# Attention and a gated feed-forward block on one core: nine x tiles transposed by DMA instead of TensorE, and SP's queue in source order

## The chip, the core and the metric

The kernel runs on one core of a Trainium2 chip. A core has five engines that run side by side, each with a queue of its own that it works through in order: TensorE (PE in the profile, with its weight loads as PEld), VectorE (DVE), ScalarE (ACT), GpSimd (POOL) and SyncE (SP). They meet by semaphores: an instruction waits until another engine or a transfer has counted one up. Transfers between the chip's memory (HBM) and the core's (SBUF) are issued by SP, ACT or POOL and carried out by 16 DMA engines. TensorE writes to PSUM, from where VectorE or ScalarE fetch its results.

The metric is the device time of the kernel in microseconds. Before the change it is 335.49 us, the median of three runs (335.31 to 337.4).

## What is computed

Attention with a sliding window over q, k and v of (8 batches, 8 heads, 576 positions, 64), then a gated feed-forward block on its output:

```python
scores = q @ k.T / sqrt(64) + slope[h] * -(i - j)      # only where 0 <= i - j < 128
attn   = softmax(scores)                                # over j
x      = (attn @ v) transposed to (4608 tokens, 512)    # 512 = 8 heads x 64
g      = x @ w_gate                                     # 512 -> 1536
out    = (g * sigmoid(g) * (x @ w_val)) @ w_out         # 1536 -> 512
```

Inputs and output are float32; the matrix products are made in float16 with float32 sums.

## The kernel before

**Units and blocks.** The attention is cut into 36 units of 128 queries. Two batches make a super-unit of nine units (p = 0 to 8): four of the first batch, four of the second, and p = 8 for the last 64 positions of both. The rank of a k, q or v tile is the number of the unit whose positions it holds. Scores of a unit read the k tile of its own rank and the q tiles of its own and the next rank (the window reaches over two tiles); units p = 3 and 7 have no next tile in their batch, and p = 7 of a later super-unit also makes a part of the ninth unit and so reads q of p = 8. The feed-forward block runs over nine blocks of 512 tokens: block n takes x of four units (block 3 takes units 13 to 16, block 4 units 18 to 21, block 5 units 22 to 25), block 8 the four ninth units.

**One unit.** `scores(i)` makes products of k and q on TensorE (lines 289 and 325), ScalarE takes the exponential (295, 329), VectorE multiplies by the mask (301, 333). `weighted(i)` multiplies by v on TensorE (357) and VectorE divides by the sums (360, 361), which leaves x with tokens across the partitions. The feed-forward products need x, k and q with the feature across the partitions, so all three are transposed.

**Transposing.** q and k up to rank 10 go through TensorE (`transposed`, line 215) and are fetched from PSUM by VectorE or ScalarE; from rank 11 on (`QK_DMA_FROM`) SP issues one transposing transfer for each (line 236). x of units 0 to 21 goes through TensorE, four transposes into one PSUM tile (line 385), and is copied to xT by VectorE or ScalarE (387, 389); from unit 22 on (`X_DMA_FROM`) SP issues a transposing transfer (line 379).

**Loads.** POOL issues all loads of q, k and v (lines 188 and 182), in an order written out by hand: after unit i those of rank i+7. They land in natural tiles, five each for q and k, which come free when the transpose has read them; v has 12 tiles, kT 12 and qT 9 places. The x tiles number three, the xT tiles three.

**Feed-forward.** `gate_val` makes the gate and value products of blocks 0 to 5 (line 413), with an activation (431) and two products on VectorE (432, 443). The projection of block 0 is a plain product (`project`, 467, fetched by ScalarE at 471); that of the later blocks is made with seven products in place of eight (`strassen`, 548). A half block of it yields two output tiles: the last write of the first is VectorE's at line 553, that of the second ScalarE's at 589, and SP stores each of them (459). Blocks 6 to 8 make their gate products with seven products too (637).

**What sets the order.** `everything` interleaves steps of the feed-forward block with steps of the attention. A scheduler then places the instructions of an engine, except where the engine is put under `manual_schedule`: there they keep the order in which the source gives them. POOL is so from the start, TensorE in the first steps and from step 60 on (about 90 us), SP never. `ahead(i)`, called after `weighted(i)` and the loads, emits transposing transfers of q and k for the units to come, from a list `order` in which `need[i]` says how many entries unit i needs:

```python
            if not late or i == last:
                weighted(i)
                yield i
            loads_to(i + 7)
            ahead(i)
```

After that x of the unit is transposed; from unit 13 to 21 that is put off by one unit, so that TensorE need not wait for VectorE.

Of the kernel before, what the change touches and what calls it, by code (L numbers as in the profile page):

```python
# [16 lines left out]
P = 128  # L17
WIN = 128
QK_DMA_FROM = 11
X_DMA_FROM = 22  # L20
MASKS_AT = (3.0, 5.0, 6.0, 7.0)
ALONE = 8
MANUAL = "compute"
ET = mybir.EngineType
# [4 lines left out]
LEAD = 6  # L29
# [21 lines left out]
def kernel(  # L51
# [92 lines left out]
    def busy(n):  # L144

        t_ = ps_f.tile([P, 512], FP32, name="nil", tag="po", bufs=1)
        for _ in range(n):
            nc.tensor.matmul(t_, idle[:, 0:P], idle, start=True, stop=True)
# [13 lines left out]
    last = len(units) - 1  # L162
# [60 lines left out]
    order = []  # L223
# [4 lines left out]
    need = [18 * s + n for s in range(NSUP) for n in (3, 5, 7, 8, 11, 13, 15, 18 if s else 16, 18)]  # L228
# [108 lines left out]
    def weighted(i):  # L337

        s, p = units[i]
        x = xpool.tile([P, H, D], FP16, name="x", tag="x")  # L340
        xs[i] = x
        for half in range(2):
            pool, tag = (ps_f, "gv") if i < FIRST else (ps_a, "a")
            av = pool.tile([P, 4, D + 1], FP32, name="av", tag=tag)
            todo = []
            for j in range(4):
                h = 4 * half + j
                if p == 8:
                    for n, kt in enumerate((3, 7, 8)):
                        todo.append((j, ex[(s, "c", n)][:, slot(h), :], va[9 * s + kt][:, h, 0:D + 1]))  # L350
                else:
                    if p not in (0, 4):
                        todo.append((j, ex[(s, p - 1)][:, slot(h), 128:256],
                                     va[9 * s + p - 1][:, h, 0:D + 1]))
                    todo.append((j, ex[(s, p)][:, slot(h), 0:128], va[9 * s + p][:, h, 0:D + 1]))
            for n, (j, w, val) in enumerate(todo):
                nc.tensor.matmul(av[:, j, :], w, val, start=(n == 0), stop=(n == len(todo) - 1))  # L357
            rec = xpool.tile([P, 4, 1], FP32, name="rec", tag="rec", bufs=4)
            with tc.high_priority() if i in (6, 7) else ExitStack():
                nc.vector.reciprocal(rec, av[:, :, D:D + 1])  # L360
                nc.vector.tensor_mul(x[:, 4 * half:4 * half + 4, :], av[:, :, 0:D],  # L361
                                     rec.broadcast_to([P, 4, D]))
# [8 lines left out]
    def x_transposed(i):  # L371
        n, j = place(i)
        if n not in xT:
            xT[n] = bpool.tile([P, NKB, 512], FP16, name="xT", tag="xTc" if n == 8 else "xT",
                               bufs=1 if n == 8 else 3)
        x = xs.pop(i).rearrange("p h d -> p (h d)")
        dst = xT[n][:, :, j * P:(j + 1) * P]
        if i >= X_DMA_FROM:
            nc.sync.dma_start_transpose(dst, x)
            return  # L380
        pool, tag, n = ((ps_f, "gv", 3) if i == 2 else (ps_f, "po", 1) if i < FIRST
                        else (ps_a, "a", 4))
        pt = pool.tile([P, NKB, P], FP16, name="px", tag=tag, bufs=n)
        for kb in range(NKB):
            nc.tensor.transpose(pt[:, kb, :], x[:, kb * P:(kb + 1) * P], idm if i < FIRST else idm2)  # L385
        if i < FIRST:
            nc.vector.tensor_copy(dst, pt)
        else:
            nc.scalar.copy(dst, pt)
# [416 lines left out]
    loaded = done_t = 0  # L806

    def loads_to(r):
        nonlocal loaded
        while loaded <= min(r, NR - 1):  # L810
            load(loaded)
            loaded += 1

    def transposes_to(n):
        nonlocal done_t
        while done_t < n:
            transpose(done_t)
            done_t += 1

    def ahead(i):  # L820

        n = need[min(i + 4, last)]
        while done_t < n and order[done_t][1] < loaded and order[done_t][1] >= QK_DMA_FROM:
            transposes_to(done_t + 1)

    def run(steps):
        for fs in steps:
            for f in fs:
                f()
            yield  # L830
# [7 lines left out]
    def first_tiles():  # L838

        first_masks()  # L840
        transposes_to(1)
        begin_scores(0, 0, 0)
        transposes_to(2)
        begin_scores(0, 0, 1)
        transposes_to(need[0])
        begin_scores(0, 1, 0)
        begin_scores(0, 1, 1)
        begin_scores(1, 0, 0, ps_f, "gv", 3)
        for n, _ in enumerate(run(scores(0))):
            if n == 0:  # L850
                begin_scores(1, 0, 1, ps_f, "gv", 3)
                transposes_to(need[1])
        for i in range(FIRST):
            if i + 1 < FIRST:
                for n, _ in enumerate(run(scores(i + 1))):
                    if n == 0 and i == 0:
                        begin_scores(2, 0, 0)
                        begin_scores(2, 0, 1)
                    if n == 0 and i + 2 < FIRST:
                        transposes_to(need[i + 2])  # L860
            else:
                later_masks()
                for m in range(2):
                    wide(0, m, "g", P)
            weighted(i)
            if 0 < i < FIRST - 1:
                x_transposed(i - 1)
        x_transposed(2)
        begin(4, 2)
        x_transposed(3)  # L870
        begin(4, 3)

    def attention():

        waiting = []
        transposes_to(need[FIRST])
        for _ in run(scores(FIRST)):
            yield FIRST
        for i in range(FIRST, last + 1):
            late = i >= LATE  # L880
            if i < last:
                transposes_to(need[i + 1])
                for n, _ in enumerate(run(scores(i + 1))):
                    yield i - len(waiting)
                    if n == 2 and late:
                        weighted(i)
                        yield i - len(waiting)
# [5 lines that stand above are left out]
            yield i - len(waiting)  # L893
            if late and i < X_DMA_FROM:
                if waiting:
                    x_transposed(waiting.pop(0))
                waiting.append(i)
                yield i
                yield i
                continue  # L900
            while waiting:
                x_transposed(waiting.pop(0))
            x_transposed(i)
            yield i
            yield i + 1
# [9 lines left out]
    queue = ExitStack()  # L915
# [40 lines left out]
    loaded = 11  # L956
# [3 lines left out]
    done = n_att = 0  # L960
# [16 lines left out]
    def progress(steps):  # L977
        total = 0.0
        for size in steps:
            total += size  # L980
            yield total

    def everything():
        nonlocal done
        base = 0
        busy(WARM)
        with tc.manual_schedule(engines=ENGINES[MANUAL]):
            first_tiles()
            done = FIRST
            steps = progress(ffn())  # L990
            while (at := next(steps)) < ALONE:
                if at == 2.0:
                    nc.scalar.copy(idm2, idm)
                if at in MASKS_AT:
                    make_mask(MASKS_AT.index(at))
        fixed = ExitStack()
        for step in steps:
            if step >= FIXED_FROM and fixed is not None:
                fixed.enter_context(tc.manual_schedule(engines=ENGINES["pe"]))
                fixed, held = None, fixed  # L1000
            b1 = 24 + 3 * PRE

            lead = LEAD if done < 22 else LEAD + 4
            blk = (0 if step + LEAD < b1 else 1 if step + LEAD < 60
                   else min(NBLK - 1, 2 + int((step + lead - 60) // 34.5)))
            if step < b1:

                target = base + 1.25 * max(0, step - ALONE) + 1.5 * max(0, step - 16)
            elif step < 60:
                target = base + 32 + SECOND * 8 * (step - b1) / (60 - b1)  # L1010
            else:
                target = 84 + (step - 57) * RATE / 34.5
            most = n_att + 2 if step >= 60 else 1000
            while (n_att < min(target, most) or done < ready[blk]) and att_step():
                pass
        held.close()

    everything()
    queue.close()

# [29 lines left out]
```

## Time and profile before

| | |
|---|---|
| median of three runs | 335.49 us (335.31 to 337.4) |
| span of the profiled execution | 333.9 us, first to last instruction, 7719 instructions |
| between that span and the median | 1.6 us |
| granted TensorE clock | full, in all of the span |
| attention | ends at about 226 us, when the last x goes out |
| blocks 2, 3, 4, 5 begin on TensorE at | 90.0, 128.5, 166.1, 202.8 us |
| TensorE's transposes of x, line 385 | 88 instructions, 14.1 to 148.5 us |
| ScalarE's copies to xT, line 389 | 18, 585 ns each |
| SP's transposing transfers | 25 of k, 25 of q, 14 of x |

The page of the profile gives for each engine its busy time and its share of the span, then the span in 40 slices of 8.35 us with a digit for the busy tenths. PEclk is the clock that TensorE was granted. The DMA row is the mean busy share of the 16 DMA engines. In a list of waits a row reads: the instruction that waited and its line, the arrow, what ended the wait, then the total in us, how often, and the longest. In a timeline a row reads: start in us, length in us, engine, line, operation, output and inputs, shape, and how many instructions are merged. SP's instructions bear a q, since they only issue; how long a transfer takes is told apart, from issue to landing.

### The profile page before, as it was taken

Reading aid. Unit: us, or ns where it says so; the run is one execution under the profiler, and the core shown is the slowest. Engines: PE = TensorE matmul, PEld = TensorE weight load, DVE = VectorE, ACT = ScalarE, POOL = GpSimd, SP = SyncE. Lnnn points to the kernel's source line nnn. Section 1 sums busy time; section 2 is a strip of 40 time slices with the busy share of each in tenths; the row PEclk is TensorE's granted clock in tenths of the full one; section 3 lists DMA queues with packets and bytes.
Section 4 is the critical chain, followed back from the end, with each engine's and each line's share of the span. In section 5 each row is a group of like instructions: output and inputs, shape, how many; then the busy total and the mean of one; then the engine's idle time right before and its main releaser. Section 6 shows DMA issues by size and latency. Waiting matters only on the chain.

```text
span 333.9 us, 7719 instructions
## 1 busy us (share of the span) xinstructions
PE 325.9 (98%) x2955; PEld 218.5 (65%) x2955; DVE 274.2 (82%) x643; ACT 206.9 (62%) x413; POOL 111.0 (33%) x138
## 2 busy tenths in 40 slices
PE   8999999999999999999999999999999999999994
PEld 4665465544465655656655655666788888888883
DVE  4678878999797879988999999999855985775683
ACT  4976777464766657567456465563567667776650
POOL 8977776458964098551035000000000000000000
PEclk9999999999999999999999999999999999999999
DMA  9999999999999999999969532030100101011014
GB/s 154 175 179 175 177 185 164 122 142 184 141 170 159 140 195 162 160 168 155 179 128 152 117 34 81 16 96 17 65 29 36 64 2 65 25 41 65 0 65 127
DMA packets 161669, 37.64 MB, mean 113 GB/s; under 512 B 149472, under 2 KB 157280, under 8 KB 161632
## 3 DMA queue, kind: packets, MB, share of 16 engines
q0 software_dynamic: 118880, 18.62, 78.8%
q1 hardware_dynamic: 42064, 17.90, 27.8%
q10 hardware_dynamic: 688, 0.62, 0.6%
q8 instruction: 23, 0.38, 0.5%
q14 instruction: 14, 0.11, 0.1%
HBM read 37.91 MB, written 9.44 MB: 142 GB/s over the span
## 4 chain that ended last, share of the span: by engine, by line
PE 87%; DVE 8%; ACT 2%; issue 1%; DVEq 0%
PE po L548 19%; PE pg L413 17%; PE pv L413 16%; PE gX L637 9%; PE av L357 5%; PE gY L637 5%; PE ps L289 3%; PE p L548 3%; PE gZ L637 2%; DVE uu L432 2%; PE psc L325 2%; DVE hT L443 2%; PE po L467 2%; PE px L385 2%; DVE ex L301 1%
## 5 line engine op out<-in xcount | busy, mean ns | idle before, releaser
L413 PE MATMUL pv<-xT,wv_sb 128*128 128x512 f16 (+2 forms) x312 | 76.6, 363 | 0.3 <-DVE uu L432 0.2
L413 PE MATMUL pg<-xT,wg_sb 128*128 128x512 f16 (+2 forms) x324 | 76.5, 355 | 0.1
L431 ACT ACTIVATE tt<-pg 128x512 f16<-128x512 f32 x68 | 40.9, 603 | 44.6 <-PE pg L413 44.6
L295 ACT ACTIVATE ex<-ps 128x512 f16<-128x512 f32 x96 | 50.0, 608 | 7.4 <-PE ps L289 7.4
L432 DVE SCALAR_TENSOR_TENSOR uu<-tt,pg 128x512 f16<-128x512 f16 x67 | 45.6, 681 | 8.6 <-ACT tt L431 8.3
L443 DVE TENSOR_TENSOR hT<-uu,pv 128x512 f16<-128x512 f16 x68 | 46.2, 681 | 1.6
L182 POOL DMA_DIRECT2D va<-in_v_dram x40 | 34.5, 871 | 38.2 <-DMA out_dram<-osb 20.4
L548 PEld LDWEIGHTS <-hT 128*128 128x128 f16 x384 | 37.2, 98 | 10.7 <-issue 0.8
L413 PEld LDWEIGHTS <-wg_sb 128*128 128x128 f16 x324 | 28.5, 98 | 23.5 <-issue 2.2
L413 PEld LDWEIGHTS <-wv_sb 128*128 128x128 f16 x312 | 27.8, 98 | 24.4 <-issue 2.3
L188 POOL DMA_DIRECT2D kn<-in_k_dram x39 | 33.5, 863 | 18.8 <-DMA qT<-qn 6.2
L188 POOL DMA_DIRECT2D qn<-in_q_dram x39 | 33.6, 871 | 9.7 <-DMA va<-in_v_dram 4.7
L548 PEld LDWEIGHTS <-S 128*128 128x128 f16 x288 | 27.5, 98 | 7.5 <-issue 1.4
L301 DVE TENSOR_TENSOR ex<-ex,m_reg 128x1024 f16<-128x1024 f16 x42 | 28.5, 685 | 3.0 <-ACT ex L295 3.0
L361 DVE TENSOR_TENSOR x<-av,rec 128x256 f16<-128x256 f32 x72 | 28.5, 420 | 0.5
L548 PE MATMUL po<-T,S 128*128 128x256 f16 x192 | 25.9, 273 | 0.3 <-ACT u2s L574 0.3
L548 PE MATMUL po<-T,hT 128*128 128x256 f16 x192 | 26.0, 272 | 0.0
L329 ACT ACTIVATE exc<-psc 128x512 f16<-128x512 f32 x40 | 21.4, 608 | 3.2 <-PE psc L325 3.1
L691 DVE TENSOR_TENSOR hT<-s,v 128x512 f16<-128x512 f16 x18 | 7.6, 424 | 17.7 <-ACT s L690 17.7
L357 PEld LDWEIGHTS <-ex 128*128 128x128 f16 x384 | 17.5, 98 | 4.4 <-issue 1.0
L357 PE MATMUL av<-va,ex 128*128 128x65 f16 x384 | 19.3, 193 | 0.3 <-ACT ex L295 0.3
L289 PE MATMUL ps<-qT,kT 64*128 64x256 f16 x192 | 16.0, 272 | 0.9 <-DVE qT L220 0.6
(129 smaller groups left out, 534.1 us busy)
## 6 DMA issues: line engine op xcount, KB each, us to landing
out_dram<-osb SPq DMA_DIRECT2D x32, 256.0 KB, 2.4
va<-in_v_dram POOLq DMA_DIRECT2D x32, 128.0 KB, 6.9
qn<-in_q_dram POOLq DMA_DIRECT2D x31, 128.0 KB, 7.9
kn<-in_k_dram POOLq DMA_DIRECT2D x31, 128.0 KB, 7.3
wg_sb<-in_moe_w_gate_dram POOLq DMA_DIRECT2D x6, 256.0 KB, 7.6
wo_sb<-in_moe_w_out_dram POOLq DMA_DIRECT2D x3, 512.0 KB, 8.2
wv_sb<-in_moe_w_val_dram POOLq DMA_DIRECT2D x5, 256.0 KB, 7.6
kn<-in_k_dram POOLq DMA_DIRECT2D x8, 64.0 KB, 6.4
```

What stands on the lines that cost most here:

```text
L182: nc.gpsimd.dma_start(va[rank][p0:p1, :, 0:D], src)
L188: nc.gpsimd.dma_start(t_[p0:p1], src)
L295: nc.scalar.activation(e[:, o:o + 2, :], banks[q4][par], AF.Exp, scale=scale)
L301: nc.vector.tensor_mul(e[:, o, :], e[:, o, :], reg[:, o, :])
L357: nc.tensor.matmul(av[:, j, :], w, val, start=(n == 0), stop=(n == len(todo) - 1))
L361: nc.vector.tensor_mul(x[:, 4 * half:4 * half + 4, :], av[:, :, 0:D], rec.broadcast_to([P, 4, D]))
L413: nc.tensor.matmul(ps[:, c0:c1], w[:, kb, ms], xT[n][:, kb, c0:c1], start=(kb == 0 and c0 == 0), stop=(kb == NKB - 1 and c1 == 512), skip_ ...
L431: nc.scalar.activation(tt, pg[:, c0:c1], AF.Tanh, scale=0.5)
L432: nc.vector.scalar_tensor_tensor(out=uu, in0=tt, scalar=one if (n, m) == PIN else 1.0, in1=pg[:, c0:c1], op0=ALU.add, op1=ALU.mult)
L443: nc.vector.tensor_mul(hT[n][:, m, c0:c1], acted[(n, m)][1][:, c0:c1], pv[:, c0:c1])
L548: nc.tensor.matmul(dst, a[:, m, cols], b[:, m, :], start=(start and m == 0), stop=(m == HM - 1), skip_group_check=True)
L637: nc.tensor.matmul(dst[:, i, :], w[:, kb, c0 + i * P:c0 + (i + 1) * P], a[:, kb, :], start=(start and i == 0 and kb == 0), stop=(i == 1 an ...
```

## The change

Three edits. x of units 13 to 21 is transposed by a transfer from SP's queue, where TensorE and ScalarE did it. `ahead(i)` emits q and k of whole ranks up to i+4, where it emitted the entries that the scores of unit i+4 need. And from unit 12 on SP's instructions keep the order of the source, where the scheduler placed them. A constant in `everything` (22) is replaced by `X_DMA_FROM`, by which the number of steps that the attention is held ahead of a block becomes 10 instead of 6 for units 13 to 21 (from 22 on it was 10 already).

```diff
 QK_DMA_FROM = 11
-X_DMA_FROM = 22
+X_DMA_FROM = 13
+AHEAD = 4
+QUEUE_FROM = 12
...
     def ahead(i):
 
-        n = need[min(i + 4, last)]
-        while done_t < n and order[done_t][1] < loaded and order[done_t][1] >= QK_DMA_FROM:
+        while (done_t < len(order) and order[done_t][1] <= min(i + AHEAD, loaded - 1)
+               and order[done_t][1] >= QK_DMA_FROM):
             transposes_to(done_t + 1)
...
         for i in range(FIRST, last + 1):
             late = i >= LATE
+            if i == QUEUE_FROM:
+                queue.enter_context(tc.manual_schedule(engines={ET.SP}))
             if i < last:
                 transposes_to(need[i + 1])
...
-            lead = LEAD if done < 22 else LEAD + 4
+            lead = LEAD if done < X_DMA_FROM else LEAD + 4
```

`x_transposed(i)` branches on `X_DMA_FROM`: at and above it, it is one `nc.sync.dma_start_transpose(dst, x)`. The branch of `attention` that puts x off by one unit holds for units from 13 up to `X_DMA_FROM`, so it is not taken any more.

## The prediction

> **What bounds the kernel now.** I read the page's busy times first, then its slices, then the waits of TensorE, then those of SP's queue.
>
> ```profile
> PE 325.9 (98%) x2955; PEld 218.5 (65%) x2955; DVE 274.2 (82%) x643; ACT 206.9 (62%) x413; POOL 111.0 (33%) x138
> ...
> PEclk9999999999999999999999999999999999999999
> DMA  9999999999999999999969532030100101011014
> ```
>
> TensorE is busy for 325.9 of 333.9 us at full clock; nothing else is near its whole span. The DMA row says that transfers are dense up to about 180 us and thin after that. In the list of TensorE's own waits no row is longer than 1.2 us in total, and that one is the start of the kernel; the only wait for a transposed q or k is this:
>
> ```profile
> PE ps L289 <- DVE qT L220: 0.6, 2, 0.4
> ```
>
> So the time is the sum of what stands in TensorE's queue. An edit gains what it takes out of that queue, and loses what makes TensorE wait. SP's queue is where waiting happens now, at no cost:
>
> ```profile
> SPq L236 <- DMA kn<-in_k_dram: 85.7, 20, 55.2
> SPq L459 <- DVE osb L553: 84.3, 11, 11.8
> ```
>
> The first row is SP waiting for k to be loaded before it can transpose it (one of these waits, 55.2 us, is the start), the second is SP waiting for an output tile.
>
> **What is removed.** x of units 13 to 21 is transposed by four TensorE instructions each, 36 in all, and a ScalarE copy each, 9 in all. One instruction's row says 219 ns, but they overlap; what counts is how far the next one is pushed. TensorE's timeline:
>
> ```profile
> 104.25 1.03 PE L413 MATMUL pv<-xT,wv_sb 128*128 128x512 f16 x4
> 105.12 0.39 PE L385 MATMUL px<-idm,x 128*128 128x128 f16 x4
> 105.34 0.82 PE L548 MATMUL po<-wo_sb,S 128*128 128x256 f16 x6
> ```
>
> From the start of the four to the start of the next group it is 0.22 us. At the other units it is the same: 0.23 at 98.57 us, 0.22 at 111.91, 118.27, 124.81, 130.93 and 135.98, 0.23 at 142.45 and 148.33. Nine times 0.22 to 0.23 is **2.0 us off TensorE**, all on the path, since nothing is waited for there. The nine copies (585 ns each, 5.3 us of ScalarE) gain nothing: ScalarE is busy 62% and its longest wait is for TensorE (44.6 us).
>
> [...] The rows above show 0.056 us per block in a full queue. [...]
>
> **What is added.** Nine transposing transfers on SP (about 1.2 us of SP's time each, 10.8 us). SP then has three per unit of about 6 us, 3.6 us, and about 0.7 us of stores: it fits. Their landing is far from its reader. Block 3 begins at 128.54 us on TensorE and reads x of units 13 to 16; x of unit 16 is ready at 111.4 us, goes out at about 113 behind q and k of rank 20, and at the slowest landing in the trace, 8.9 us, is there at 122. Block 4 begins at 166.07 and its last x (unit 21) is ready at 142.1. So 6 us and more are spare; cost nothing, and if that cover went, the gate products of block 3 would wait for the difference. The x tiles (three) are free again well before their third successor three units later.
>
> **What is moved: SP's queue.** The built queue of the changed kernel runs, from rank 17 on: q and k of rank r, then x of unit r-4, and between these the two stores of each half block. In the built queue of before, x of unit 22 stands behind k of rank 33; now it stands behind rank 26. The source's own limit changes by one rank at most; it is the scheduler's hoisting that goes. Instructions of POOL stand in the same order, those of TensorE too but for the 36 transposes, so the new `lead` moves nothing there.
>
> What is now queued behind a waiting instruction: a store waits for its output tile, and behind it stand q and k of the next rank, which the scores three units on read. I take for each rank the moment that releases SP, add SP's issues (1.3 us a transposing transfer with its gap, 0.5 to 0.6 a store), and compare with the start of the first scores that need q. The two rows that matter most, release and need, on VectorE and TensorE:
>
> ```profile
> 124.89 0.41 DVE L553 SCALAR_TENSOR_TENSOR osb<-po,u2s 128x256 f32<-128x256 f32 x1
> ...
> 137.16 0.96 PE L289 MATMUL ps<-qT,kT 64*128 64x256 f16 x8
> ```
>
> - q of rank 23 (unit 22 reads it): tile ready 125.3; store, k22, q22, x of 18, store, so q23 goes out at 130.3. Need 137.16: 6.9 us. Need moves forward by seven removed groups, release by four: **6.2 us** are left for the landing.
> - q of rank 26 (unit 25): the ScalarE output copy at line 589 ends at 148.05; store, k26, so q26 goes out at 149.9. Need 156.07; less one removed group: **5.9 us**.
> - The others the same way, release first: q17 (output copy at line 471 ends at 88.3), out 90.2, need 99.76, less one group: 9.3. q20 (line 589 at 109.9), out 110.5, need 120.11, less two: 9.2. q24 (behind q23, k23 and x of 19), out 134.2, need 143.64, less three: 8.8. q29 (line 589 at 165.9), 166.5 to 174.7: 8.2. q32 (185.4), 186.0 to 192.1: 6.1. q35 (202.5, then k35), 204.4 to 210.3: 5.9.
>
> Against these stands the time from issue to landing:
>
> ```profile
> DMA to landing us min/median/max: 2.4/6.5/8.9
> ```
>
> This is line 236 as a whole. In parts: 6.3 to 8.9 (median 7.6) at 128 to 140 us, while POOL issues loads without a break; 2.5 to 4.8 at 57 to 62 and 3.5 to 5.2 at 156 to 160, when POOL stands still; x of units 27 to 35 lands in 2.4 to 4.0. q32 and q35 come when the loads are over (the last lands at 185.4): no stall. The ranks with more than 8 us cannot stall either. Only q23 and q26 are open. Bounds: at 2.4 us nothing, at 8.9 us 2.7 + 3.0 = **5.7 us of stall**; below nothing there is no end, since TensorE has no such wait now that could go.
>
> I take **about 5 us, so no stall**, and this is the choice that the forecast hangs on. The natural tiles of q and k have five buffers, so the load of rank r waits until rank r-5 is transposed. In before the transposes run far ahead (k of rank 23 goes out at 111.75, when TensorE has just scored unit 17), so POOL runs ahead too and seven loads are in flight at 130 us. Now, when q23 goes out, rank 22 has not landed, so the loads of rank 27 can't have begun, and those up to 26 have been out since about 119 to 127 us. That is nearer to the rows with POOL at rest. The same bursts that SP sends after a store find the loads held back by the very ranks that are late. The price of it, later loads, is covered: a load lands within 8 us (median of q), and rank r's load starts about two units before SP comes to it.
>
> **The sum**, against the profiled execution: span 333.9 - 2.0 + 0 = 331.9 us. The median of the runs, 335.49, lies 1.6 us above that span, which I leave as it is: **333.5 us**, 0.6% faster. About 1% is what a measurement of this kernel can tell from no change, so this counts as the same.
>
> **Rivals.**
> 1. *Part of the gain is eaten.* q23 and q26 land in 6.5 to 7.1 us, as the loaded rows' lower half. Stall at 7: 0.8 + 1.1 = 1.9, time 335.4. For it: the median of line 236 is 6.5. Against: the loads held back.
> 2. *Slower: the two stores hold back q23 and q26 in a full DMA queue.* The mechanism is the one above, with landing at 8.9 us at both: -2.0 + 5.7 = +3.7, **339.2 us**. It is slower than before from a landing of 7.1 us on. For it: nine more transfers of 128 KB in a stretch whose DMA row is all nines, and 8.9 was seen with 7 loads and 4 transfers of SP in flight. Against: the bytes that are added are 1.2 of 37.64 MB, and loads no longer run ahead.
> 3. *The change does less than it says.* The 36 transposes are gone from the built queue, so this can only be that they cost nothing where they stood: 335.5. The timeline speaks against it at nine places.
>
> **The numbers.** Forecast 0.60 (its own range 333.0 to 334.3), first rival 0.20 (334.3 to 336.0), second 0.15 (from 336.0 up, 339.2 at its price), third 0.05. Of the second I put 0.09 above 338.8, which is slower by over 1%. Faster by over 1% means below 332.1; TensorE's whole list of waits has little more to give, 0.03, out of the forecast's share. The range 332.8 to 337.5 leaves out a few hundredths below, and some 0.11 above, where the bound of 339.2 lies.
>
> **What would show it.** TensorE's px group has 52 instead of 88 instructions, the ScalarE copy at that place 9 fewer; 23 x transfers. Right: no wait of TensorE for a q or k transfer at the scores of units 22 and 25, landings of 4 to 6 us around 130 and 150 us, POOL waiting for transposed q and k between ranks. Wrong: a row of TensorE's weight loads or scores waiting for the transfer into qT, of 1 to 3 us, near 135 and 154 us. What would make the forecast wrong altogether is a landing above 7 us there, or a stall at places where I found over 8 us.

## The result and the profile after

The changed kernel takes **334.02 us** (median of 16 runs, 333.72 to 335.22), the kernel before 335.59 us (16 runs, 334.94 to 337.4). The ratio is 0.9947, with a 95% interval of 0.9932 to 0.9963: a gain of 1.6 us (by the interval 1.2 to 2.3), clear of noise. The forecast was 333.5 us in a range of 332.8 to 337.5. The gain that it named was 2.0 us; 1.6 came. It also held that about 1% is the least that can be told from no change; with 16 runs on each side half of that could be told.

First the busy times and the DMA row of the page of the changed kernel (its line numbers are two higher than before), which answer to those of before:

```profile
PE 324.5 (97%) x2919; PEld 216.6 (65%) x2919; DVE 273.4 (82%) x643; ACT 202.5 (61%) x404; POOL 111.1 (33%) x138
...
DMA  9999999999999999999999664231100101011014
```

TensorE has 36 instructions fewer and 1.4 us less of busy time, ScalarE has lost its nine copies and 4.4 us of busy time. The DMA row stays dense for two slices longer: what was loaded early is loaded later now. The spans of the two profiles (333.9 and 333.0) can't be subtracted as they stand, because the profiled execution of the changed kernel was 0.62 us later already when its first transposes were done, long before anything that the change touches. What counts is how the distance between the two moves after that.

At the place that the prediction showed, TensorE's timeline of the changed kernel reads:

```profile
104.65 1.03 PE L415 MATMUL pv<-xT,wv_sb 128*128 128x512 f16 x4
105.51 0.82 PE L550 MATMUL po<-wo_sb,S 128*128 128x256 f16 x6
106.17 1.03 PE L415 MATMUL pg<-xT,wg_sb 128*128 128x512 f16 x4
```

From the start of the value products to that of the projection it is 0.86 us; before, with the four transposes between, 1.09. Laid side by side, instruction by instruction, the two TensorE queues differ in time by these steps after the start, and by no other as large:

| where (time before) | step of the changed kernel against before |
|---|---|
| nine groups of four transposes, 98.6 to 148.3 us | -0.22 us each, -2.0 in all |
| scores of unit 22, 137.2 us | +0.65 us |
| scores of unit 25, 156.3 us | +0.24 us |
| scores of unit 28, 175.3 us | -0.24 us |
| sum | -1.4 us |

The second row is a wait that the prediction did not see. TensorE's timeline of the changed kernel there, then VectorE's, then VectorE's before:

```profile
135.26 1.03 PE L415 MATMUL pv<-xT,wv_sb 128*128 128x512 f16 x4
136.22 0.39 PE L291 MATMUL ps<-qT,kT 64*128 64x256 f16 x4
137.12 0.72 PE L291 MATMUL ps<-qT,kT 64*128 64x256 f16 x4 [0.51 <-DVE x L363]
```

```profile
135.49 0.41 DVE L505 TENSOR_TENSOR S<-hT 128x512 f16<-128x512 f16 x1
135.83 0.68 DVE L335 TENSOR_TENSOR exc<-exc,m_reg 128x1024 f16<-128x1024 f16 x1
136.43 0.24 DVE L362 RECIPROCAL rec<-av 128x4 f32<-128x4 f32 x2
136.63 0.76 DVE L363 TENSOR_TENSOR x<-av,rec 128x256 f16<-128x256 f32 x2
```

```profile
136.71 0.24 DVE L360 RECIPROCAL rec<-av 128x4 f32<-128x4 f32 x2
136.92 0.76 DVE L361 TENSOR_TENSOR x<-av,rec 128x256 f16<-128x256 f32 x2
```

The scores need four PSUM tiles, and the pool has four. Two of them still hold the sums of unit 20, which VectorE has yet to divide; it does so from 136.6 to 137.4 us, after other work that stands before it in its queue. TensorE came 0.94 us earlier than before, VectorE's division only 0.29, and the second half of the scores waits: the group takes 1.62 us, from 136.22 to 137.84. Before, the same scores took 0.96 us where 0.61 is their length without a wait, so 0.35 us of this wait was there already. It stood in the list of the weight loads, as one of the two waits of this row (at 137.7 us; the other, at 175.3, is at the scores of unit 28):

```profile
PEld L289 <- DVE x L361: 0.5, 2, 0.2
```

The third row is the landing of q of rank 26. It went out at 149.4 us and landed 155.7; the second half of unit 25's scores, which read it, could have begun at about 155.6. TensorE's timelines show the group at 0.87 us in the changed kernel, at 0.62 before, and at 0.65 in a second profiled execution of the changed kernel ("changed, measured again" in the experiments), in which the same q went out at 148.3 us and landed at 154.3, just in time:

```profile
155.34 0.87 PE L327 MATMUL psc<-qT,kT 64*128 64x128 f16 x16
156.07 0.62 PE L325 MATMUL psc<-qT,kT 64*128 64x128 f16 x16
154.16 0.65 PE L327 MATMUL psc<-qT,kT 64*128 64x128 f16 x16
```

The fourth row is a wait of before, again for VectorE's x, that has gone. The scores of unit 28 in the changed kernel, before, and in the second execution of the changed kernel:

```profile
174.20 0.70 PE L291 MATMUL ps<-qT,kT 64*128 64x256 f16 x8
174.71 0.94 PE L289 MATMUL ps<-qT,kT 64*128 64x256 f16 x8
172.81 0.93 PE L291 MATMUL ps<-qT,kT 64*128 64x256 f16 x8
```

The third and the fourth row belong together: where TensorE has lost 0.24 us at unit 25, it comes to unit 28 that much later and finds x divided; where q of rank 26 lands in time, neither step is there. The second execution has neither and ends as the first does: from the first of the nine groups to the end TensorE gains 1.35 us on before in it, 1.38 in the first. So the late q costs nothing in the end, and what is lost of the 2.0 us is the second row.

In SP's queue the waits have the same two heads as before:

```profile
SPq L461 <- DVE osb L555: 94.2, 13, 11.8
SPq L238 <- DMA kn<-in_k_dram: 61.4, 4, 55.5
```

SP now waits for a load of k only four times, where it was 20: it comes to q and k when they have long been there. POOL waits in its place. This is from POOL's list of waits, the changed kernel and then before, and below it the landing of q and k over the whole run of the changed kernel:

```profile
POOL kn L190 <- DMA kT<-kn: 31.4, 13, 4.7
POOL kn L188 <- DMA kT<-kn: 1.8, 1, 1.8
```

```profile
DMA to landing us min/median/max: 2.4/5.4/8.4
```

Thirteen loads of k were held back until the transposing transfer of five ranks earlier had freed a tile, and the median of the landing fell from 6.5 to 5.4 us.

### The profile page after: what moved, and what is told of

Its sections match the earlier page's. It is cut to its first block, busy times and chain, and to the rows that moved or that the text cites. A ratio compares the mean times of both kernels' runs of the same rounds, so it can differ in the third digit from the quotient of the medians.

```text
span 333.0 us, 7659 instructions
## 1 busy us (share of the span) xinstructions
PE 324.5 (97%) x2919; PEld 216.6 (65%) x2919; DVE 273.4 (82%) x643; ACT 202.5 (61%) x404; POOL 111.1 (33%) x138
## 4 chain that ended last, share of the span: by engine, by line
PE 85%; DVE 10%; ACT 2%; issue 1%; DVEq 0%
PE po L550 18%; PE pg L415 16%; PE pv L415 15%; PE gX L639 9%; PE gY L639 5%; PE av L359 5%; PE ps L291 3%; PE p L550 3%; DVE uu L434 2%; PE gZ L639 2%; DVE hT L445 2%; PE psc L327 2%; PE po L469 2%; DVE ex L303 1%; ACT tt L433 1%
## 5 line engine op out<-in xcount | busy, mean ns | idle before, releaser
L550 PEld LDWEIGHTS <-hT 128*128 128x128 f16 x384 | 37.1, 98 | 10.7 <-issue 0.8
```

The source lines that it names most:

```text
L550: nc.tensor.matmul(dst, a[:, m, cols], b[:, m, :], start=(start and m == 0), stop=(m == HM - 1), skip_group_check=True)
```

## Experiments

All ratios are to the kernel before, run beside each kernel on the same chip, with 95% intervals.

| kernel | median us | ratio |
|---|---|---|
| changed (first measurement) | 334.02 | 0.9947 (0.9932 to 0.9963) |
| queue alone | 335.22 | 0.9993 (0.9983 to 1.0002) |
| x alone | 348.27 | 1.0378 (1.0360 to 1.0396) |
| both ways | 335.86 | 1.0006 (0.9991 to 1.0021) |
| x of 20 and 23 early | 333.41 | 0.9949 (0.9926 to 0.9972) |
| lead of six | 334.10 | 0.9951 (0.9932 to 0.9969) |
| lead of three (two runs) | 356.12 | 1.0604 (1.0541 to 1.0666) |
| x of 20 early, lead of five | 332.81 | 0.9910 (0.9886 to 0.9934) |
| changed, measured again | 333.74 | 0.9946 (0.9926 to 0.9966) |

### SP's order without the x transfers

```diff
-X_DMA_FROM = 13
+X_DMA_FROM = 22
```

> SP's queue in source order and q and k whole ranks up to i+4, as in the changed kernel, but x of units 13 to 21 still transposed on TensorE. My theory (the gain is the 36 transposes that left TensorE's queue; the order of SP's queue is worth nothing by itself): the time of before, ratio 0.998 to 1.002, and TensorE's steps as in before. Rival (the order of SP's queue makes the gain): the time of the changed kernel, ratio 0.995. Both: fewer loads in flight than in before when q of ranks 23 and 26 go out, so their landing below 6.5 us.

Measured 335.22 us, ratio 0.9993, an interval that holds 1. TensorE's queue is that of before, and so is its time; no step of more than 0.1 us shows between the two after the start. q and k land in 3.9 to 5.3 us (median 4.7) between 128 and 140 us, against 6.3 to 8.9 before. So SP's order makes transfers faster that nobody waits for, and gains nothing by itself.

### The x transfers without SP's order

```diff
-            if i == QUEUE_FROM:
-                queue.enter_context(tc.manual_schedule(engines={ET.SP}))
...
-        while (done_t < len(order) and order[done_t][1] <= min(i + AHEAD, loaded - 1)
-               and order[done_t][1] >= QK_DMA_FROM):
+        n = need[min(i + 4, last)]
+        while done_t < n and order[done_t][1] < loaded and order[done_t][1] >= QK_DMA_FROM:
             transposes_to(done_t + 1)
```

> x of units 13 to 21 by transfer, but SP's order left to the scheduler and the old limit in ahead. x of unit 13 then stands behind k and q of rank 22 in SP's queue. My theory: it goes out at about 113 to 116 us instead of 93, x of unit 16 needs its tile (three x tiles), so VectorE is held for 3 to 6 us from 111 us on, and TensorE with it: 336 to 341 us, slower than the changed kernel by 2 us or more, ratio to before 1.00 to 1.02. Rival (x is wanted so late that any order will do): 334.0, ratio 0.995.

Measured 348.27 us: slower than the changed kernel by 14 us, where 2 to 7 were expected. The direction and the place were right, the size was not. SP's timeline has the first x of the nine (unit 13, ready at 92 us) at last here:

```profile
114.98 1.22 SPq L238 DMA_TRANSPOSE qT<-qn  x1
116.29 1.22 SPq L381 DMA_TRANSPOSE xT<-x  x1
```

It stood behind k and q of rank 23, whose loads SP had to wait for. VectorE's timeline shows the price, since x of unit 16 is to be written where x of unit 13 still lay, and TensorE's shows who waits for VectorE:

```profile
109.61 0.24 DVE L362 RECIPROCAL rec<-av 128x4 f32<-128x4 f32 x2
120.35 0.76 DVE L363 TENSOR_TENSOR x<-av,rec 128x256 f16<-128x256 f32 x2 [10.49 <-DMA xT<-x]
```

```profile
112.00 0.39 PE L291 MATMUL ps<-qT,kT 64*128 64x256 f16 x4
120.83 0.93 PE L291 MATMUL ps<-qT,kT 64*128 64x256 f16 x4 [8.44 <-DVE x L363]
```

VectorE waited 16.0 us in three such places. Another 3.1 us were lost to TensorE's clock after the long wait (below). So the two parts of the change belong together: the transfer is worth 2.0 us on TensorE, and it costs far more if x stands behind q and k that are not wanted yet.

### The transposes put back on TensorE, the transfers kept

```diff
-            if late and i < X_DMA_FROM:
+            old = xs[i]
+            x_transposed(i)
+            if late and i < 22:
                 if waiting:
-                    x_transposed(waiting.pop(0))
-                waiting.append(i)
...
+                    on_tensor(waiting.pop(0))
+                waiting.append(old)
...
```

`on_tensor` makes four transposes on TensorE into a PSUM tile that nobody reads.

> The changed kernel with the 36 transposes put back on TensorE: x of units 13 to 21 goes by transfer and is read from there, and TensorE transposes it as well, at the place of before, into a PSUM tile that nobody reads. SP's queue is that of the changed kernel; ScalarE is spared the nine copies. My theory (TensorE's time is the gain): the time of before, ratio 0.998 to 1.002. Rival (the gain comes from SP's order, or from ScalarE's nine copies of 0.585 us): 334.0, ratio 0.995.

Measured 335.86 us, ratio 1.0006. With the transposes back in TensorE's queue the gain is gone, though SP's queue is that of the changed kernel and ScalarE still has no copies to make. The gain is TensorE's time and nothing else. The steps of 0.24 us at the scores of units 25 and 28, one up and one down, are there in this kernel too (q of rank 26 landed at 156.06 us, the group took 0.88), so they don't come from the transposes that left TensorE. Nor does SP's order make them by itself: in queue alone that q landed in 2.4 us and neither step is there.

### VectorE's x of units 20 and 23 first

```diff
-            with tc.high_priority() if i in (6, 7) else ExitStack():
+            with tc.high_priority() if i in (6, 7, 20, 23) else ExitStack():
```

> The changed kernel with the division of x of units 20 and 23 put ahead of other work on VectorE (high priority, as units 6 and 7 have it); all other queues unchanged. My theory (0.65 us of the gain is lost at the scores of unit 22 and 0.24 at those of unit 25, which wait for a PSUM tile that VectorE still reads for x): these two waits go, 0.4 to 0.9 us below the changed kernel, 333.1 to 333.6, ratio to before 0.992 to 0.994. Rival (what was lost there is a transposed q that lands late): as the changed kernel, 334.0. If VectorE is full there, the wait only moves to the products that were passed: 333.6 to 334.2.

Measured 333.41 us, ratio 0.9949. The median is 0.3 to 0.6 us below those of the changed kernel, and the interval does not tell it from that kernel. The trace does: the scores of unit 22 take 0.61 us. The step of 0.65 us is gone, and with it the 0.35 us of wait that before had there, so that this wait was VectorE's. The 0.24 us at unit 25, however, stayed (and came back at unit 28), and it was not VectorE's, as the expectation had it. TensorE's weight loads between 80 and 230 us wait there for:

```profile
PEld L327 <- DMA qT<-qn: 0.2, 1, 0.2
```

That is the late q of rank 26 (landed at 154.58 us, the second half of the scores began at 154.63), one of the two places that the prediction had left open.

### A lead of six and a lead of three

```diff
-AHEAD = 4
+AHEAD = 6
```

A kernel of its own has 3 in the same place.

> The changed kernel with q and k put in six units ahead of the scores in place of four; TensorE's and VectorE's orders unchanged. My theory (with four, loads are held back by their five buffers and transfers land in 3.4 to 7.5 us; a longer lead lets POOL run ahead again and fill the DMA queues, but gives each q two units more of reserve): median landing of q and k at 128 to 140 us back above 6.3 us, and a time like the changed kernel's, 333.6 to 334.2, the 0.24 us at the scores of unit 25 gone. Rival (landing depends on how many transfers SP sends, not on the loads): landing as with four, median 5.4.

Measured 334.10 us, ratio 0.9951: as the changed kernel. The step at unit 25 is gone (q of rank 26 landed at 146.4 us, 8.7 us ahead of the scores that read it) and with it the one at unit 28; that at unit 22 is not. The landings between 128 and 140 us answer the question of the loads. This is the landing of q and k there with a lead of six, and then with a lead of three:

```profile
DMA to landing us min/median/max: 7.3/7.7/9.5
```

```profile
DMA to landing us min/median/max: 2.4/3.7/5.6
```

In the changed kernel, with four, it was 3.4/5.4/7.5, before the change 6.3/7.6/8.9. SP sends the same transfers in all of them but before, so it is the lead that sets the landing; over the whole kernels too the medians are 4.1, 5.4 and 7.5 us with three, four and six. The further SP runs ahead, the more loads POOL has in flight beside it: when these transfers went out between 128 and 140 us, there were 2.0 on average with a lead of three (only four transfers), 3.0 with four, 7.5 with six, and 7.0 before. That the loads in flight are what makes the landing long fits these numbers, but no kernel changed them alone.

> The changed kernel with q and k put in three units ahead in place of four. My theory: q of a rank then goes out about one unit before its scores; from the division of one unit to the scores two units on it is some 3.4 us, and issue and landing take about 8, so TensorE waits about 4 us in each of some 18 units: 370 to 420 us, waits of TensorE for transfers into qT. Rival (the lead has a reserve of more than a unit everywhere): 334 to 336.

Measured 356.12 us (two runs, 354.23 and 358.00), 22 us more than with four, where 36 and more were expected. TensorE's list of waits, from the run of 354.23, has the cause as named, at ten places and not at 18:

```profile
PE ps L291 <- DMA qT<-qn: 17.7, 10, 4.8
```

TensorE's granted clock was lower in this kernel too: 0.97 on average from 90 to 155 us and 0.95 from 155 to 190, where the changed kernel has 1.00. If it was 0.50 where it was not full, as in x alone, these means make an estimated 3.9 and 3.5 us at half clock, which cost up to 2.0 and 1.8 us more. The landing itself is shorter with so short a lead, which the expectation left out; that a wait makes the next unit later and so gives its q more time is the likely rest of the miss, not tested by itself. Four is the least lead that works here, and the forecast stood close to an edge.

### Both waits taken away

```diff
-AHEAD = 4
+AHEAD = 5
...
-            with tc.high_priority() if i in (6, 7) else ExitStack():
+            with tc.high_priority() if i in (6, 7, 20) else ExitStack():
```

> The changed kernel with x of unit 20 put ahead on VectorE and q and k put in five units ahead. My theory: both places go at which TensorE was held back in the changed kernel (0.65 us at the scores of unit 22 by VectorE, 0.24 us at those of unit 25 by the landing of q of rank 26): 0.5 to 0.9 us below the changed kernel run beside it, 332.9 to 333.5. Rival (landing gets longer with the lead and eats it): as the changed kernel, 334.0.

> The changed kernel itself, on the chip of the runs beside it. Both theories: 333.7 to 334.3, ratio to before 0.993 to 0.997.

Measured 332.81 us (332.63 to 333.11) beside 333.74 us (333.55 to 334.53) for the changed kernel on the same chip: 0.9 us less, and no run of the one reaches the other's. The ratio to before is 0.9910. TensorE's timeline at unit 22 has no wait left:

```profile
134.49 1.03 PE L415 MATMUL pv<-xT,wv_sb 128*128 128x512 f16 x4
135.45 0.61 PE L291 MATMUL ps<-qT,kT 64*128 64x256 f16 x8
```

The scores take 0.61 us here, 1.62 with their wait in the changed kernel and 0.96 before. The group at unit 25 is back at 0.62. This version beats both kernels; the landings in it are long (7.1 to 9.0 at 128 to 140 us), and each q has a unit more to land in. The gain over the changed kernel is that of x of unit 20: the 0.65 us that the change lost there and the 0.35 that before lost. The longer lead has no share in it that can be shown: the wait at unit 25 was given back at unit 28 anyway, and counted in the same way TensorE gains 2.15 us on before with x of 20 and 23 early and a lead of four, and 2.28 here.

## Why the prediction was right, step by step

- **The 36 transposes, 2.0 us.** Right to the second digit: nine steps of 0.22 us in TensorE's queue. Putting them back (both ways) takes the gain away. One instruction's row says 219 ns; four of them pushed the next group by 0.22 us, and with the transfer in their place the kernel is faster by 1.6 us.
- **ScalarE's copies, nothing.** Right: both ways has none of them and gains nothing.
- **x lands in time.** Right in the changed kernel; x of unit 16 landed at 121.1 us and block 3 began at 128.05. The cover that the prediction named, SP's order, is what x alone takes away, but the first to suffer is not block 3: it is VectorE, which needs the x tile again. The prediction had mentioned the three tiles in passing and found them free "well before"; they are, with that order.
- **q23 and q26, about 5 us of landing, no stall.** The choice on which the forecast hung. q of rank 23 went out at 131.3 and landed in 3.4 us, ahead of its scores at 136.2. SP came to it later than counted, so 4.9 us were left and not 6.2: at the 5 us of the forecast it would have been on the edge, and that it wasn't is in part luck. (In the second execution it landed in 4.4 us, with 5.4 left.) q of rank 26 landed in 6.3 us against the 5.9 that were counted as left, and cost 0.24 us, which came back at unit 28. The reason given, loads held back by five tiles, is shown as far as the holding back goes by the waits of POOL, and the leads of three and six show the landing move with it.
- **The other ranks cannot stall.** Right for all of them.
- **"All on the path, since nothing is waited for there": the term that was mis-sized.** It was taken as -2.0 and became -1.4 in the trace, by +0.65 at unit 22. TensorE's list of waits showed no product of the scores waiting for VectorE's x, and I read from it that TensorE could come earlier by any amount. But VectorE was busy for 34.9 of the 38 us from 128 to 166 in before, and the weight loads ahead of those scores already waited 0.15 and 0.22 us for it. An engine that comes 0.9 us earlier meets an engine that doesn't. With x of unit 20 put first on VectorE the wait is gone, and the time falls to 332.81 us (with a lead of five), below the forecast.

Of the rivals, the first (part of the gain is eaten by the landing) happened at one of its two places, with a quarter of a microsecond that the end of the kernel doesn't show: part of the gain was eaten, but by VectorE. The second did not, since landing stayed below 7.1 us at both; the third is refuted by both ways.

## What to carry to other kernels

Price an instruction by how far it pushes the next one in its queue, not by its own row: 219 ns in the row were 56 in the queue. When an engine is to gain time, look at who feeds it just after, and count that one's slack, even where the lists show no wait, or only one of 0.2 us. A transfer in an in-order queue is worth what stands ahead of it: put it behind work that isn't wanted soon, and the tile that it reads stays occupied for the engine that writes the next (VectorE waited 10.5 us for one such tile in x alone).

## What the runs showed of the hardware

The time from issue to landing of a transposing transfer rose with the number of loads in flight beside it: a median of 2.4 us for x from 205 us on in the changed kernel, whose last load lands at 184.3 us, and a median of 3.7, 5.4 and 7.7 us between 128 and 140 us with leads of three, four and six, beside 2.0, 3.0 and 7.5 loads on average.

In TensorE's wait of 8.4 us in x alone its granted clock fell from 1.00 to 0.50, between 115 and 117 us. The windows of that kernel, with the granted clock behind POOL's busy time:

```profile
112.00:121.00 9.00, 0.56 (x6) 0.21 (x5) 0.65 (x2) 1.57 (x3) 0.00 (x0) 0.77 1.54 173
121.00:127.00 6.00, 6.00 (x43) 3.66 (x43) 5.03 (x12) 1.09 (x2) 0.30 (x1) 0.50 0.70 165
```

In the second window TensorE is busy throughout and granted half its clock, which cost 3.1 us: the distance to before grew from 7.5 us at the end of the wait to 10.7. Finer windows show where the clock fell and rose:

```profile
113.00:115.00 2.00, 0.00 (x0) 0.00 (x0) 0.00 (x0) 0.74 (x2) 0.00 (x0) 1.00 1.85 136
115.00:117.00 2.00, 0.00 (x0) 0.00 (x0) 0.00 (x0) 0.00 (x0) 0.00 (x0) 0.97 1.72 165
117.00:119.00 2.00, 0.00 (x0) 0.00 (x0) 0.00 (x0) 0.00 (x0) 0.00 (x0) 0.50 1.30 229
125.00:127.00 2.00, 2.00 (x28) 1.74 (x26) 1.73 (x6) 0.00 (x0) 0.30 (x1) 0.50 1.11 271
127.00:129.00 2.00, 2.00 (x12) 0.98 (x11) 0.27 (x2) 0.98 (x2) 2.00 (x3) 0.97 0.49 38
```

If the clock takes no value between the 1.00 and the 0.50 of these windows, a mean of 0.97 over 2 us is 0.12 us at half clock. By this estimate it fell at about 116.9 us, 4.5 us after the last product, and rose at about 127.1, 6.3 us after the first product behind the wait (120.8 us); half clock lasted 10.2 us, 3.9 us of it inside the wait. What sets these times was not shown: it is one wait of this length in one kernel.
